# A new instruction order for an agent-attention and maxout-FFN kernel, with w_out loaded ahead of the second batch's keys

## The chip, the cores and the metric

The kernel runs on one core of one Trainium2 chip. The metric is the device time of one execution in microseconds (us), and less is better. Each time is a median over several executions on the chip.

The core has five engines, each with its own instruction stream that runs in order: TensorE (PE, matmuls; its weight loads are listed as PEld), VectorE (DVE), ScalarE (ACT), GpSimd (POOL) and SyncE (SP). SP computes nothing here: it issues all large DMA transfers, and its order is the order in which they enter the queue.

## What is computed

Two layers follow each other. Agent attention: 4 batches of 12,544 tokens with 128 channels; 49 agents per batch first gather from keys and values, then the queries read from the agents. After that comes a feed-forward layer whose hidden units are the maximum of three products.

```python
def sm(a, b):
    s = scale * (a @ b.transpose(0, 2, 1))
    s = s - s.max(-1, keepdims=True)
    e = np.exp(s)
    return e / (e.sum(-1, keepdims=True) + 1e-09)
a2k = sm(agents, k)
agent_v = a2k @ v
q2a = sm(q, agents)
x = (q2a @ agent_v).reshape(B * S, D)
...
h = np.maximum(np.maximum(x @ w1, x @ w2), x @ w3)
return (h @ w_out).astype(np.float32)
```

w1, w2 and w3 are 128 x 768, w_out is 768 x 128. Inputs and output are float32; the kernel multiplies in bfloat16.

## The kernel before

**Algebra.** The queries' side never forms x. For each batch the kernel multiplies the 49 agent values by w3 - w1 and w2 - w1 and by w1 times w_out once (the tile G), and each query tile's 49 exponentials then go straight to the hidden units. The maximum of three becomes a linear part and two ReLU-like steps.

**Steps.** The function `graph` names every step. Its names are used below, with a batch b and a chunk g for keys and values (12 chunks in batch 0, 11 in each later one), or a query tile s (49 tiles of 1,024 queries, so-called superblocks) and a sixth f of the hidden units.

- SP: `kl`, `vl` load a chunk of keys or values; `ql.s` a tile of queries; `lw..` half of a weight; `lwo` w_out; `st.s` stores a result tile; `kt` (batches 1 to 3) and `qd.s` transpose cast keys or queries by DMA.
- POOL: `kc`, `vc`, `qc` cast what was loaded to bfloat16 (L335, L517), `cwo` casts w_out (L405), `ea` sums exponentials (L474).
- PE: `ks` key scores (L359), `kv` exponentials times values (L376), `qt.s` transposes queries where DMA does not (L523), `sc.s` query scores (L533), `su` their sums (L545), `u.s.f` and `v.s.f` the two products for a sixth of the hidden units (both L558, two matmuls each, on half of the array's rows at a time), `li` the linear part (L582), `p.s.o.f` the output product (L592, four matmuls each), `pl` w1 times w_out (L417).
- ACT: `kx` and `ex` exponentials (L365, L539), `a.s.f` the first ReLU (L571, and L565 for f = 4), `x.s.4` (L568).
- DVE: `x.s.f` the maximum (L574), `ov` scales by the reciprocal sums and fills a result tile (L599), `qe` evacuates transposed queries (L527), `nr` normalises a batch's agent values (L428 for batch 0).

On PE the steps are of three kinds, set by the `mode` in `graph`: `u` and `v` use half of the rows (49 agents in each half), `sc` and the products for G half of the columns, all others the full array.

**Stages.** Batch 0's keys and values come first; its G is ready at some 41 us. From then on the superblocks 0 to 48 follow each other, overlapped, and the key and value chunks of batches 1 to 3 ride on the superblocks ahead of their own (batch 1 on superblocks 1 to 11, batch 2 on 12 to 22, batch 3 on 24 to 34).

**What sets the order.** Nothing is scheduled when the kernel is built: a string, `ORDER`, lists all 2,889 steps, and the function `run` issues them one after the other, each on its engine. A word is a step and, behind the slash, the buffers that its new tiles take; a step waits, beside its inputs, for the last reader of what its buffer held. The number of buffers is fixed:

```python
SLOTS = {"UV": 3, "OM": 2, "LD": 13, "QB": 3, "KB": 3, "VB": 4, "KT": 3, "QT": 3, "EQ": 4, "EK": 4, "AS": 3,
         "R": 13, "RC": 4, "OS": 9, "G": 4, "VA": 2, "EA": 2, "ES": 2, "KR": 2}
```

LD holds loaded chunks, tiles and weights; KB, VB and QB their casts; KT and QT what was transposed; EK and EQ exponentials; UV and OM are in PSUM, the matmuls' output; R holds hidden units, OS result tiles.

```python
for name in order:
    o = plan.ops[plan.index[name]]
    for t in o["new"]:
        self.new(plan.tiles[t], t)
    o["fn"]()
```

Of the kernel before, what the change touches and what calls it, by code (L numbers as in the profile page):

```python
# [25 lines left out]
TURNED = (*range(13, 36, 2), 26, 32, *range(36, 49))  # L26
# [89 lines left out]
def graph(plan, em):  # L116
# [93 lines left out]
    for s in range(NQ):  # L210
# [433 lines left out]
kl0.5/0 prep kl0.0/1 kl0.9/2 kl0.1/3 kl0.6/4 vl0.0/5 vl0.11/6 ql.0/7 kl0.2/8 kl0.10/9 kl0.7/10 kc0.1/0 vl0.5/11 kc0.9/1 kt0.1/0  # L644
lw3a/12 kc0.5/2 vl0.7/3 kc0.0/0 kt0.5/1 kl0.4/2 ke0.5/0 kc0.6/2 vl0.9/0 ke0.1/1 ks0.5/1 qc.0/0 kt0.0/2 kx0.5/0 kl0.8/1 vc0.0/0
kl0.11/4 qt.0/0 ke0.0/0 ks0.1/1 qe.0/0 ks0.0/2 kc0.7/0 kl0.3/7 kx0.1/1 kt0.6/0 vc0.5/1 vl0.6/5 sc.0/0 ke0.6/0 kc0.2/2 vl0.8/10
kt0.7/1 ex.0/0 kt0.2/0 ke0.7/1 vc0.7/2 vl0.10/11 ks0.7/1 kx0.0/2 kc0.4/2 vl0.2/8 kx0.7/3 kt0.9/2 wm.0/1 wm.1/1 vc0.11/3 kc0.10/0
ke0.9/1 vl0.4/3 vd0.11 ks0.9/2 ke0.2/2 to0.0/0 to0.7 kv0.0 vl0.3/9 kc0.8/1 kt0.10/0 to0.5 vc0.9/0 ks0.2/1 ke0.10/1 vl0.1/6 kv0.5
kt0.4/0 kc0.11/0 kx0.9/0 kv0.7 ke0.4/2 kx0.2/2 lw1a/2 kc0.3/2 to0.2 ks0.6/0 ks0.4/1 kx0.6/3 kt0.3/2 lw2a/4 vc0.6/2 kt0.8/0 to0.6
ke0.8/2 kv0.6 lw1b vc0.8/1 ke0.3/0 ks0.8/0 to0.9 lw3b kv0.9 vc0.10/2 kt0.11/2 to0.1 kx0.8/0 ke0.11/2 to0.8 vd0.10 kv0.8 lw2b  # L650
# [4 lines left out]
ex.1/1 x.0.5/1 kc1.2/1 qt.2/1 x.0.4/2 vl1.0/9 u.0.0/0 ql.3/8 qe.2/0 v.0.3/1 a.0.0/2 vl1.1/10 u.1.5/2 x.0.3/3 sc.2/1 gl/0 a.1.5/0  # L655
v.0.0/0 kc1.1/2 x.0.0/4 u.0.2/1 gvl v.1.5/2 a.0.2/1 li.0.0/0 kt1.1/2 p.0.0.3 x.1.5/5 p.0.0.1 ex.2/2 u.1.3/0 v.0.2/1 a.1.3/2
p.0.0.5 kt1.2/0 x.0.2/6 ks1.0/1 p.0.0.0 u.1.2/2 kx1.0/1 v.1.3/0 vc1.0/0 a.1.2/0 kl1.3/5 p.0.0.4 x.1.3/7 u.2.5/1 vl1.2/3 p.0.0.2
a.2.5/1 su.1 kl1.4/11 kv1.0 qc.3/0 u.1.1/2 ov.0.0/0 ql.5/9 v.1.2/0 a.1.1/2 vl1.4/2 u.1.4/1 re.1/1 va1.0/0 x.1.2/8 li.0.1/0 qt.3/1
kl1.8/8 vc1.1/0 a.1.4 p.0.1.4 u.1.0/2 qe.3/0 v.1.1/0 qc.4/0 a.1.0/0 v.1.4 x.1.1/2 p.0.1.1 vl1.3/4 p.0.1.5 p.0.1.3 x.1.4/0 p.0.1.2
p.0.1.0 u.2.3/0 ov.0.1 u.2.4/2 a.2.3/2 v.1.0/1 ks1.1/1 x.1.0/4 li.1.0/0 p.1.0.2 a.2.4 su.2 p.1.0.3 p.1.0.5 re.2/0 v.2.5/0 kx1.1/0  # L660
u.2.1/1 v.2.4 x.2.5/6 a.2.1/0 p.1.0.4 kv1.1 p.1.0.1 p.1.0.0 x.2.4/3 va1.1 v.2.1/0 ov.1.0/1 v.2.3/1 vc1.2/0 sc.3/1 x.2.3/1 u.2.2/2
ex.3/0 li.1.1/0 p.1.1.4 kc1.3/1 a.2.2/1 p.1.1.2 x.2.1/0 ks1.2/1 p.1.1.0 v.2.2/1 kx1.2/3 kc1.4/2 u.2.0/2 kt1.3/0 p.1.1.5 x.2.2/4
a.2.0/2 kv1.2 su.3 p.1.1.1 p.1.1.3 kl1.5/11 u.3.5/0 re.3/2 va1.2 v.2.0/1 ov.1.1 vl1.5/5 a.3.5/1 u.3.1/2 li.2.0/1 ql.6/3 x.2.0/7
p.2.0.3 p.2.0.4 kl1.6/6 a.3.1/0 qt.4/0 ql.7/10 u.3.4/0 qe.4/0 kt1.4/2 u.3.3/1 a.3.4 v.3.5/2 p.2.0.5 x.3.5/2 p.2.0.2 p.2.0.0
a.3.3/2 vc1.3/0 p.2.0.1 kl2.1/12 sc.4/0 ov.2.0/2 v.3.4 ex.4/1 v.3.3/2 ea1.0/0 v.3.1/1 x.3.4/5 x.3.3/8 li.2.1/1 vl2.0/7 p.2.1.5
ks1.3/0 su.4 p.2.1.4 kx1.3/1 x.3.1/6 u.3.2/0 u.4.5/2 a.3.2/2 kv1.3 p.2.1.3 kc1.5/1 p.2.1.0 va1.3 re.4/1 v.3.2/1 a.4.5/0 u.3.0/0
# [197 lines left out]
```

## Time and profile before

| | us |
|---|---|
| three runs | 447.28, 449.17, 452.19 |
| median | 449.17 |
| the profiled execution | 448.96 |
| its span, first to last instruction | 447.1 |

The page of the profile gives busy times by engine, 40 slices of the span, DMA queues and the costliest groups of instructions. The timeline gives stretches of instructions merged by group: start, duration, engine, line, operation, output and inputs, shapes, count, and in brackets the idle time of the engine before it with what ended it. "issue" is idle time for which the profile shows no wait. PE's matmuls overlap, and their ends are modelled, so that a group's pace is read from start to start. KB are 1,024 bytes.

From records of the waits, the engines' longest in total:

```
engine line waited for: us in total, times, longest us
POOL QB L517 <- DMA LD<-in_q_dram: 50.3, 8, 11.9
POOL KB L335 <- DMA LD<-in_k_dram: 42.8, 13, 8.4
PEld L592 <- issue: 41.1, 149, 0.6
POOL QB L517 <- DMA QT<-QB: 35.6, 8, 10.1
```

### The profile page before, as it was taken

To read this page: it belongs to the slowest core of one execution; us is meant where nothing else is said; L and a number is where in the kernel's file an instruction comes from. 1 tells how busy PE (TensorE), PEld (TensorE's weight loads), DVE (VectorE), ACT (ScalarE), POOL (GpSimd) and SP (SyncE) were. 2 spreads that over 40 slices of the span, in tenths; PEclk is the share of its full clock that TensorE was granted. 3 is DMA by queue.
4 is the path that set the end of the run, shared out by engine and by line. 5 is a ranking of instruction groups with operands and counts; after the bars stand their busy time and mean duration, and the time that the engine had idled before them with its cause. 6 is when DMAs were issued, how large, how long until landed. Compare 5 with 4: busy or idle time off the path is not lost.

```text
span 447.1 us, 12853 instructions
## 1 busy us (share of the span) xinstructions
PE 421.8 (94%) x5260; PEld 270.8 (61%) x5260; DVE 392.1 (88%) x496; ACT 393.6 (88%) x461; POOL 169.5 (38%) x176
## 2 busy tenths in 40 slices
PE   0787899999999999999899999999999999999996
PEld 0554466666666666666566666666665555655675
DVE  1345799999999999999899999998999999999996
ACT  1469799999999999999889999999999999999983
POOL 1641645555694222824871324527601201000000
PEclk9989699999999999999999999999999999999999
DMA  8999999999999999999999999999699464450405
GB/s 312 410 408 387 346 372 281 298 405 308 327 291 307 352 285 285 345 310 225 321 354 253 313 302 345 303 221 353 189 300 282 103 189 122 90 195 22 164 37 202
DMA packets 97045, 121.98 MB, mean 273 GB/s; under 512 B 70423, under 2 KB 73179, under 8 KB 96987
## 3 DMA queue, kind: packets, MB, share of 16 engines
q1 hardware_dynamic: 96784, 121.07, 90.4%
q8 instruction: 41, 0.67, 0.6%
q14 instruction: 17, 0.14, 0.1%
q10 hardware_dynamic: 203, 0.10, 0.1%
HBM read 78.74 MB, written 25.69 MB: 234 GB/s over the span
## 4 chain that ended last, share of the span: by engine, by line
PE 83%; DMA 8%; DVE 3%; issue 2%; POOL 2%; ACT 1%; SPq 1%; DVEq 0%; POOLq 0%
PE UV L558 35%; PE OM L592 31%; PE OM L582 6%; DMA LD<-in_v_dram 4%; PE OM L533 3%; DVE R L574 2%; PE OM L523 2%; DMA LD<-in_k_dram 2%; PE OM L376 2%; PE OM L359 2%; DMA LD<-in_q_dram 1%; PE OM L545 1%; SPq L325 1%; DVE OS L599 1%; POOL QB L517 1%
## 5 line engine op out<-in xcount | busy, mean ns | idle before, releaser
L574 DVE TENSOR_TENSOR R<-UV,AS 128x1024 bf16<-128x1024 f32 x245 | 293.4, 1219 | 17.8 <-PE UV L558 12.9
L571 ACT ACTIVATE AS<-UV 128x1024 bf16<-128x1024 f32 x245 | 246.3, 1024 | 17.8 <-PE UV L558 13.5
L558 PE MATMUL UV<-EQ,G 49*128 49x512 bf16 (+1 forms) x1248 | 181.7, 371 | 0.9
L592 PE MATMUL OM<-wo_bf,R 128*128 128x128 bf16 x2352 | 180.4, 220 | 0.0
L592 PEld LDWEIGHTS <-R 128*128 128x128 bf16 x2352 | 139.8, 98 | 43.4 <-issue 41.1
L558 PEld LDWEIGHTS <-G 49*128 49x128 bf16 x1248 | 61.5, 94 | 61.8 <-issue 21.7
L517 POOL CAST QB<-LD 128x1024 bf16<-128x1024 f32 x49 | 51.1, 1048 | 98.4 <-DMA LD<-in_q_dram 50.3
L335 POOL CAST KB<-LD 128x1152 bf16<-128x1152 f32 (+2 forms) x45 | 49.7, 1116 | 60.4 <-DMA LD<-in_k_dram 42.8
L599 DVE TENSOR_TENSOR OS<-OM,RC 128x512 f32<-128x512 f32 x98 | 67.1, 684 | 3.6 <-PE OM L592 2.5
L335 POOL CAST VB<-LD 128x1152 bf16<-128x1152 f32 (+1 forms) x33 | 37.3, 1137 | 47.7 <-DMA LD<-in_v_dram 14.7
L565 ACT ACTIVATE UV<-UV 128x1024 f32<-128x1024 f32 x49 | 49.8, 1017 | 2.5 <-PE UV L558 1.2
L568 ACT ACTIVATE R<-UV 128x1024 bf16<-128x1024 f32 x49 | 50.1, 1023 | 1.7 <-PE UV L558 1.2
L582 PE MATMUL OM<-G,EQ 128*128 128x256 bf16 x196 | 37.9, 276 | 0.0
L539 ACT ACTIVATE EQ<-OM 128x512 bf16<-128x512 f32 x49 | 29.5, 602 | 0.9 <-PE OM L533 0.6
L474 POOL TENSOR_TENSOR EA<-EA,EK 128x441 f32<-128x441 f32 x27 | 27.6, 1023 | 4.8 <-ACT EK L365 4.1
L347 DVE COPY KT<-UV 128x1152 bf16<-128x1152 bf16 (+1 forms) x12 | 8.2, 700 | 17.3 <-PE UV L342 17.3
L582 PEld LDWEIGHTS <-EQ 128*128 128x128 bf16 x196 | 12.6, 97 | 15.6 <-issue 14.2
L533 PE MATMUL OM<-QT,agT 128*64 128x512 bf16 (+1 forms) x104 | 20.4, 398 | 0.2 <-DMA QT<-QB 0.2
L365 ACT ACTIVATE EK<-OM 128x441 bf16<-128x441 f32 (+1 forms) x33 | 17.8, 540 | 2.9 <-POOL EA L474 1.6
L376 PE MATMUL OM<-EK,VB 128*128 128x49 bf16 x392 | 17.3, 186 | 2.7 <-ACT VB L333 1.4
L359 PEld LDWEIGHTS <-KT 128*128 128x128 bf16 x392 | 14.6, 98 | 7.5 <-issue 4.5
L376 PEld LDWEIGHTS <-VB 128*128 128x128 bf16 x392 | 14.3, 97 | 7.9 <-issue 5.0
(67 smaller groups left out, 186.1 us busy)
## 6 DMA issues: line engine op xcount, KB each, us to landing
LD<-in_q_dram SPq DMA_DIRECT2D x48, 512.0 KB, 6.4
out_dram<-OS SPq DMA_DIRECT2D x48, 512.0 KB, 5.6
LD<-in_k_dram SPq DMA_DIRECT2D x40, 576.0 KB, 7.3
LD<-in_v_dram SPq DMA_DIRECT2D x40, 576.0 KB, 8.7
LD<-in_k_dram SPq DMA_DIRECT2D x3, 512.0 KB, 9.0
LD<-in_v_dram SPq DMA_DIRECT2D x3, 512.0 KB, 8.1
LD<-in_moe_w_dram SPq DMA_DIRECT2D x6, 192.0 KB, 8.4
KT<-KB SPq DMA_TRANSPOSE x33, 7.0
```

What stands on the lines that cost most here:

```text
L335: (self.nc.gpsimd if eng == POOL else self.nc.vector).tensor_copy(out=out, in_=src)
L376: self.nc.tensor.matmul(out, vb[:, j, :], e[:, j * A:(j + 1) * A], start=False, stop=True, skip_group_check=True)
L517: return lambda: self.nc.gpsimd.tensor_copy(out=self.t[f"qb.{s}"], in_=self.t[f"q.{s}"][:, :GT, :])
L533: self.nc.tensor.matmul(self.t[f"qs.{s}"][h * H:(h + 1) * H, jj * P:(jj + pairs) * P], self.agT[:, b, :], self.t[f"qT.{s}"][:, 2 * jj + h: ...
L558: self.nc.tensor.matmul(t[:, h, jj * P:(jj + pairs) * P], self.t[f"G{b}"][h * H:h * H + A, c + f * P:c + (f + 1) * P], self.t[f"e.{s}"][h ...
L565: return lambda: self.nc.scalar.activation(self.t[f"u.{s}.{f}"], self.t[f"u.{s}.{f}"], AF.Relu)
L568: return lambda: self.nc.scalar.activation(self.t[f"r.{s}.{f}"], self.t[f"u.{s}.{f}"], AF.Relu)
L571: return lambda: self.nc.scalar.activation(self.t[f"a.{s}.{f}"], self.t[f"u.{s}.{f}"], AF.Relu)
L574: return lambda: self.nc.vector.tensor_tensor(out=self.t[f"r.{s}.{f}"], in0=self.t[f"v.{s}.{f}"], in1=self.t[f"a.{s}.{f}"], op=ALU.max)
L582: self.nc.tensor.matmul(self.t[f"o.{s}.{o}"][:, i * 2 * C:(i + 1) * 2 * C], self.t[f"e.{s}"][:, jj * P:(jj + 1) * P], self.t[f"G{of[jj]}"] ...
L592: self.nc.tensor.matmul(self.t[f"o.{s}.{o}"][:, c:c + C], self.t[f"r.{s}.{f}"][:, h, jj * P:(jj + 1) * P], self.wo_bf[:, f, :], start=Fals ...
L599: self.nc.vector.tensor_tensor(out=self.t[f"os.{s}"][:, j:j + 4, :], in0=self.t[f"o.{s}.{o}"].rearrange("p (j c) -> p j c", c=C), in1=self ...
```

## The change

The operations, their engines and sizes and the number of buffers stay as they are; so does which query tiles are transposed by DMA (`TURNED` is only written with other spaces). The string `ORDER` is replaced: the steps stand in another order, and many take other buffers. The last 271 words are the same. The part around the end of batch 0 and the start of the superblocks, before and after:

```diff
@@ -641,195 +641,196 @@
 ORDER = """
-kl0.5/0 prep kl0.0/1 kl0.9/2 kl0.1/3 kl0.6/4 vl0.0/5 vl0.11/6 ql.0/7 kl0.2/8 kl0.10/9 kl0.7/10 kc0.1/0 vl0.5/11 kc0.9/1 kt0.1/0
-lw3a/12 kc0.5/2 vl0.7/3 kc0.0/0 kt0.5/1 kl0.4/2 ke0.5/0 kc0.6/2 vl0.9/0 ke0.1/1 ks0.5/1 qc.0/0 kt0.0/2 kx0.5/0 kl0.8/1 vc0.0/0
...
-vc0.2/0 su.0/1 ks0.3/2 ks0.11/0 kx0.4/0 kv0.2 ql.1/11 vc0.4/1 to0.4 ks0.10/1 kx0.3/2 kv0.4 kl1.0/8 kx0.11/3 to0.3 kx0.10/0 vc0.3/1
-to0.10 to0.11 wm.2/2 wm.3/0 wm.4/1 rc0/0 lwo/3 vc0.1/0 kv0.3 kv0.11 ql.2/9 d31a kv0.10 d21a kl1.2/10 kv0.1 wm.5/2 wm.6/0 cw1
-ql.4/6 nr0/0 d31b kl1.1/5 gpa/1 gpc/0 wm.7/2 gva d32 gpb/2 gvc u.0.1/1 gvb tw1/0 a.0.1/0 d21b qc.1/0 u.0.3/2 ew1 gpd/0 a.0.3/1
-u.0.5/1 gvd cwo qt.1/0 re.0/0 a.0.5/2 v.0.1/0 kc1.0/0 qe.1/0 u.0.4/2 pl/1 x.0.1/0 a.0.4 v.0.5/1 qc.2/0 kt1.0/1 sc.1/0 el v.0.4
...
+kx0.10/1 ke0.4/1 ks0.4/1 vc0.6/0 to0.10 ks0.2/0 kv0.6 kx0.2/0 ex.0/0 to0.2 kv0.2 kx0.8/2 kt0.3/0 vl0.1/4 lw3a/0 lw1a/3 lw1b
+lw2a/11 lw3b lw2b ql.1/6 qc.1/0 lwo/12 cwo ql.2/5 qc.2/1 vc0.8/2 to0.8 wm.0/2 wm.1/2 kv0.8 vc0.10/0 vd0.10 kx0.4/0 vc0.4/2 ke0.3/0
...
+to0.3 wm.3/1 wm.4/2 wm.5/0 rc0/0 d31a cw1 kv0.3 kv0.10 wm.6/1 wm.7/2 kv0.1 nr0/0 gpa/0 gva d21a gpc/1 gvc d31b u.0.1/0 a.0.1/0 d32
...
```

So SP's queue around w_out changes from `ql.1 kl1.0 lwo ql.2 kl1.2 ql.4 kl1.1 kt1.0 vl1.0` to `ql.1 lwo ql.2 vl1.0 kl1.1 kl1.0 kl1.2 vl1.2 ql.3 vl1.1 kt1.0`. Further on the two orders differ in which loads, stores and transposes SP issues first, for instance ahead of the last transpose of batch 2's keys (`kt2.10`): `kt2.9 qd.21 ql.24 st.14 vl3.5 st.13 kt2.10` before, `vl3.0 ql.23 vl3.2 st.4 ql.26 kt2.10` after; in where POOL's `ea` sums stand among the casts; and in how `u`, `v`, `p` and the small steps alternate on PE.

More of the change, by code (lines that the diff above doesn't have):

```diff
@@ L25 @@
 LATER = [KT] * 10 + [8]
-TURNED = (*range(13, 36, 2), 26, 32, *range(36, 49))
+TURNED = (*range(13,36,2),26,32,*range(36,49))
 PE, ACT, DVE, POOL, SP = range(5)
@@ L728 @@
-p.18.1.5 a.19.0/2 p.18.1.3 p.18.1.0 va2.8 u.20.3/2 ov.18.1 v.19.0/0 kl3.2/8 a.20.3/0 u.20.4/1 x.19.0/7 su.20 li.19.0/1 p.19.0.2
-kc3.0/1 st.9 p.19.0.3 a.20.4 p.19.0.1 re.20/2 u.20.1/2 v.20.5/0 vc3.1/0 a.20.1/2 v.20.4 x.20.5/4 p.19.0.5 kt3.0/2 p.19.0.4
-p.19.0.0 x.20.4/9 vc2.10/2 sc.21/0 ov.19.0/6 v.20.3/2 u.20.2/0 ex.21/0 v.20.1/1 ea2.6 x.20.3/8 ks2.9/1 a.20.2/1 li.19.1/0 p.19.1.4
-ea2.7 p.19.1.5 x.20.1/5 su.21 p.19.1.2 kx2.9/2 u.21.3/0 v.20.2/2 qc.23/2 a.21.3/0 kv2.9 x.20.2/1 u.20.0/1 p.19.1.3 vc3.2/1
@@ new lines @@
+kt2.5/0 re.14/0 va2.2 u.14.5/2 a.14.5/2 st.12 vl2.6/7 vc2.3/1 u.14.4/1 a.14.4 li.13.0/0 p.13.0.2 p.13.0.3 p.13.0.1 st.10 v.14.5/2
+x.14.5/9 u.14.1/0 a.14.1/0 sc.15/1 ex.15/1 ea2.0/0 vc2.4/2 ea2.1 ea2.2 p.13.0.4 p.13.0.5 p.13.0.0 ov.13.0/3 v.14.4 x.14.4/7
+v.14.3/2 x.14.3/6 v.14.1/0 x.14.1/0 ks2.3/1 su.15 kx2.3/0 li.13.1/0 p.13.1.0 p.13.1.3 vl2.7/6 kl2.9/3 kl2.6/12 vl2.5/0 vc2.5/0
+u.14.2/1 kc2.6/1 a.14.2/1 u.14.0/2 a.14.0/0 p.13.1.5 p.13.1.1 kv2.3 va2.3 re.15/2 v.14.2/0 x.14.2/2 u.15.5/1 a.15.5/2 p.13.1.4
@@ new lines @@
+p.14.1.5 ov.14.1 u.16.4/0 a.16.4 v.15.0/1 x.15.0/9 kt2.6/1 u.16.5/2 a.16.5/2 sc.17/1 ex.17/2 kt2.9/2 li.15.0/0 p.15.0.3 p.15.0.2
+p.15.0.1 v.16.5/1 ql.22/10 v.16.4 x.16.4/6 u.16.2/2 a.16.2/0 qc.19/2 qd.19/0 vl2.9/11 p.15.0.4 p.15.0.5 x.16.5/7 p.15.0.0
+ov.15.0/2 ks2.5/1 v.16.3/1 x.16.3/0 u.16.1/0 su.17 li.15.1/0 ea2.3 kc2.8/0 ea2.4 vc2.6/2 p.15.1.0 p.15.1.3 a.16.1/2 v.16.1/2
+x.16.1/5 u.16.0/1 u.17.5/0 p.15.1.4 p.15.1.2 kx2.5/2 kv2.5 re.17/0 va2.5 a.16.0/1 a.17.5/2 ea2.5 vc2.8/0 p.15.1.5 p.15.1.1 ov.15.1
@@ new lines @@
+u.17.4/1 v.16.2/2 x.16.2/4 li.16.0/1 p.16.0.5 p.16.0.1 v.16.0/0 x.16.0/8 a.17.4 v.17.4 x.17.4/1 u.17.3/2 a.17.3/0 kc2.7/2 vc2.7/1
+qt.18/0 qe.18/1 p.16.0.4 v.17.5/1 x.17.5/3 u.17.1/0 a.17.1/1 p.16.0.0 p.16.0.3 p.16.0.2 ov.16.0/0 sc.18/0 ex.18/1 v.17.3/2
+x.17.3/9 u.17.2/0 a.17.2/2 v.17.1/1 x.17.1/2 ks2.6/0 kx2.6/2 li.16.1/1 p.16.1.0 ea2.6 qc.20/2 p.16.1.1 qc.22/0 u.17.0/0 a.17.0/0
+v.17.2/2 x.17.2/5 kv2.6 p.16.1.5 vc2.9/2 kc2.10/1 su.18 va2.6 re.18/2 u.18.5/1 a.18.5/1 v.17.0/0 x.17.0/7 st.9 p.16.1.3 p.16.1.2
@@ new lines @@
+x.21.5/0 sc.22/1 ex.22/0 p.20.0.2 p.20.0.5 p.20.0.0 ov.20.0/4 u.21.1/1 a.21.1/2 v.21.3/2 x.21.3/8 u.21.2/0 a.21.2/1 li.20.1/1
+p.20.1.4 kt2.10/0 ks2.10/0 v.21.1/1 x.21.1/2 p.20.1.2 kx2.10/3 ql.24/2 vc2.10/0 ea2.7 u.22.5/2 a.22.5/0 v.21.2/0 x.21.2/5 p.20.1.0
+p.20.1.3 u.21.0/1 a.21.0/2 kv2.10 su.22 qc.23/1 vc3.1/2 ea2.8 ea2.9 fo2/0 to2 qd.23/0 kl3.0/0 ql.27/9 u.22.4/2 a.22.4 va2.10
+nr2/0,2 kc3.0/1 vc3.6/0 re.22/0 u.22.3/0 v.21.0/1 x.21.0/9 p.20.1.5 li.21.0/0 vl3.3/11 p.21.0.2 p.21.0.4 p.20.1.1 ov.20.1 a.22.3/1
@@ L833 @@
+p.48.1.0 ov.48.1 st.48
 """
```

349 lines of the change are left out of this document (170 added, 179 removed).

## The prediction

> **What bounds the kernel now.** I read the page's first lines, then the windows, then single stretches of the timeline.
>
> ```profile
> span 447.1 us, 12853 instructions
> ...
> PE 421.8 (94%) x5260; PEld 270.8 (61%) x5260; DVE 392.1 (88%) x496; ACT 393.6 (88%) x461; POOL 169.5 (38%) x176
> ...
> PEclk9989699999999999999999999999999999999999
> ```
>
> ```profile
> 20.00:40.00 20.00, 15.57 (x256) 10.78 (x254) 7.93 (x17) 15.29 (x23) 5.15 (x6) 0.91 1.03 403
> 41.00:58.00 17.00, 15.13 (x131) 7.31 (x130) 12.98 (x18) 13.51 (x18) 9.74 (x9) 0.80 1.09 341
> 60.00:100.00 40.00, 39.99 (x542) 26.96 (x541) 37.88 (x49) 37.87 (x46) 21.24 (x21) 1.00 1.05 339
> 180.00:220.00 40.00, 38.65 (x506) 25.45 (x507) 37.26 (x47) 37.35 (x45) 24.43 (x25) 1.00 1.10 297
> 260.00:300.00 40.00, 39.98 (x516) 25.88 (x513) 37.75 (x46) 38.07 (x46) 15.19 (x15) 1.00 1.10 300
> 320.00:340.00 20.00, 19.97 (x240) 12.41 (x238) 18.74 (x24) 17.86 (x23) 4.46 (x5) 1.00 0.96 281
> 340.00:400.00 60.00, 59.60 (x616) 33.99 (x615) 57.37 (x63) 57.25 (x64) 7.29 (x7) 1.00 0.55 145
> ```
>
> The columns of a window are its length, then busy time of PE, PEld, DVE, ACT and POOL, the granted clock, the DMA share and GB/s. Four stages stand there. Up to about 40 us the loads set the pace (DMA share 1.03 at 403 GB/s). From 41 to 58 nothing is full: ACT is idle 17.00 - 13.51 = 3.5 us, DVE 4.0 us, and the clock is 0.80. From 60 to 300 PE has hardly a gap and the DMA share in the rows shown lies between 1.05 and 1.10: two resources are full at once. After 340 the DMA share is 0.55, and PE alone is left. Whether a busy PE is really a full PE is seen in the timeline:
>
> ```profile
> 250.28 0.62 PE L592 MATMUL OM<-wo_bf,R 128*128 128x128 bf16 x8
> ...
> 250.83 0.39 PE L558 MATMUL UV<-EQ,G 49*128 49x512 bf16 x2
> 251.15 0.45 PEld L592 LDWEIGHTS <-R 128*128 128x128 bf16 x8 [0.23 <-issue]
> 251.15 0.62 PE L592 MATMUL OM<-wo_bf,R 128*128 128x128 bf16 x8
> ...
> 251.61 0.40 PE L376 MATMUL OM<-EK,VB 128*128 128x49 bf16 x9
> ...
> 251.93 0.83 PE L558 MATMUL UV<-EQ,G 49*128 49x512 bf16 x6
> ...
> 252.70 0.39 PE L582 MATMUL OM<-G,EQ 128*128 128x256 bf16 x2
> ```
>
> Read starts against starts. Eight L592 matmuls before another of the full-array kind (L376) take 251.61 - 251.15 = 0.46 us; before an L558, which uses half the rows, 250.83 - 250.28 = 0.55. One L558 pair before a full-array matmul takes 0.32; three pairs take 0.77, so that the two inner ones take (0.77 - 0.32) / 2 = 0.225. A **switch between kinds costs about 0.095 us** either way, and the rest goes from start to start with no room. PE is at its own pace here, and the count of switches is part of the time.
>
> At this point a rule stands against mine. The Trainium skill (Perfetto Trace Analysis, Identifying the Most-Contended Engine) says that matmul busy time misjudges TensorE and that weight-load busy time should be taken instead. By it PE, at 61%, would have room, ACT and DVE would be the contended engines, and the switches would cost nothing. The row with "0.23 <-issue" speaks against it here: the weight load's idle time sits inside the switch. I keep it as a rival.
>
> **The change, part by part.** *First keys and values.* Counted in the order of SP's instructions, 23 key and value loads, the first q tile and one half of w3 stand ahead of the last values; afterwards the same without w3.
>
> ```profile
> LD<-in_q_dram SPq DMA_DIRECT2D x48, 512.0 KB, 6.4
> out_dram<-OS SPq DMA_DIRECT2D x48, 512.0 KB, 5.6
> LD<-in_k_dram SPq DMA_DIRECT2D x40, 576.0 KB, 7.3
> ...
> LD<-in_moe_w_dram SPq DMA_DIRECT2D x6, 192.0 KB, 8.4
> ```
>
> At 403 GB/s a key or value load (576 KB, 0.590 MB) takes 1.46 us of the queue, a q or result tile 1.30, half a weight 0.49. The last values, their normalisation (39.64 below) and the first product over hidden units (41.15) come 0.5 us earlier: **-0.5**.
>
> *The passage into the steady state.*
>
> ```profile
> 39.64 0.21 DVE L428 TENSOR_TENSOR avT<-OM,KR 128x49 bf16<-128x49 f32 x1 [0.20 <-PE OM L376]
> ...
> 41.15 0.39 PE L558 MATMUL UV<-EQ,G 49*128 49x512 bf16 x2
> ...
> 44.56 0.83 POOL L405 CAST wo_bf<-LD 128x768 bf16<-128x768 f32 x1 [1.39 <-DMA LD<-in_moe_w_out_dram]
> 45.33 1.15 POOL L335 CAST KB<-LD 128x1152 bf16<-128x1152 f32 x1
> 45.44 0.49 PE L417 MATMUL OM<-wo_bf,w1T 128*128 128x128 bf16 x6 [1.05 <-POOL wo_bf L405]
> ...
> 46.42 1.04 POOL L517 CAST QB<-LD 128x1024 bf16<-128x1024 f32 x1
> ...
> 47.52 1.03 PE L523 MATMUL OM<-ident,QB 128*128 128x128 bf16 x8 [0.60 <-POOL QB L517]
> ...
> 49.13 1.94 ACT L571 ACTIVATE AS<-UV 128x1024 bf16<-128x1024 f32 x2 [0.99 <-PE UV L558]
> ```
>
> Now SP sends q tile 1, keys 1.0, w_out, q tile 2. Afterwards it sends q 1, w_out, q 2, then batch 1's values and keys: w_out and q 2 land one key load, 1.46 us, earlier, and the key cast at 45.33 no longer stands between the two casts on POOL that PE waits for. The three waits shown, 1.05 + 0.60 + 0.99 = 2.64 us, go; PE's wait for w_out was 1.05, less than the 1.46 gained, and next late there is DVE's evacuation of w1, ahead of which u.0.0 and v.0.5 now stand as cover. The bounds are nothing and the 3.5 us that ACT is idle, which hold the half clock's price too; I take **-2.6**, the named waits. What pays is batch 1's first transpose, which has three more key or value loads ahead of it (4.4 us). Its consumer ks1.0 stands behind 14 u, 13 v and 15 p steps instead of 8, 7 and 3: 12 pairs and 12 groups of four L592 at about 0.225 are 5.4 us of PE. That covers it; without the cover up to 4.4 us would show.
>
> *Kinds on PE.* From u.0.1 on I count 577 switches before and 597 after: 14 of the extra ones by the end of batch 2's part, 20 in all. The last 181 PE steps are the same in both. **+1.9**, of which 1.3 by 220 us.
>
> *The wait at 217.*
>
> ```profile
> 213.27 2.62 SPq L454 DMA_TRANSPOSE KT<-KB  x1
> ...
> 216.57 0.54 ACT L365 ACTIVATE EK<-OM 128x441 bf16<-128x441 f32 x1 [1.55 <-POOL EA L474]
> ...
> 217.16 0.39 PE L376 MATMUL OM<-EK,VB 128*128 128x49 bf16 x9 [1.14 <-ACT EK L365]
> ```
>
> ACT's exponentials for keys 2.9 waited for POOL, whose sum ea2.6 stood behind casts of keys and values. Afterwards ea2.6 stands about 6 us of PE steps, added up at the durations above, ahead of that use instead of 1.3, so this goes: **-1.5**. What is late next is ks2.10, the last keys of batch 2.
>
> ```profile
> 223.48 0.37 PE L359 MATMUL OM<-agT,KT 128*128 128x49 bf16 x8
> ```
>
> ```profile
> DMA to landing us min/median/max: 7.1/8.2/8.6
> ```
>
> That second row is of the KT transposes between 195 and 226 us. The one issued at 213.27 landed at about 213.27 + 8.2 = 221.5, 2.0 us before its use at 223.48. After the change PE would be there 0.5 + 2.6 + 1.5 - 1.3 = 3.3 us earlier, at 220.2. But SP has 75 key or value loads, 27 q loads and 13 stores ahead of this transpose, where it had 74, 25 and 14, with the same 26 transposes: one load of 1.46 and one tile of 1.30 more, 2.8 us. With the DMA share at 1.10 there is no idle time to put them into. So PE waits 221.5 - 220.2 = 1.3 us if the two transfers overlap the turn, and 4.1 if they delay it in full. I take the middle, **+2.7**.
>
> The sum: -0.5 - 2.6 + 1.9 - 1.5 + 2.7 = 0.0, between -1.4 and +1.4 by the last term alone. The profiled execution took 448.96 us, 1.9 above its span and 0.2 below the median of the three runs, 449.17. So the forecast is **449.0**: what the start gains, the switches and the full DMA queue give back.
>
> **The rivals.** *The lead is kept.* The transposes come in time for the earlier PE, and the gain passes 220 us without a wait: 0.0 - 2.7 = -2.7 in all, **446.3**; with the whole 3.5 us of ACT's idle time won, 445.4. For it: each transpose could be issued sooner, since SP's order around it is new. Against it: the share of 1.10.
>
> *PE has room.* By the page named above, the 1.9 us of switches are not paid: **447.1**.
>
> *The fetches.* The change weighs four places of the instruction fetches.
>
> ```profile
> q8 instruction: 41, 0.67, 0.6%
> ```
>
> These are 41 packets of 16 KB. In this profile PE's named waits after 44 us are 1.05, 0.60 and 1.14, and each has another cause, so no fetch shows. The three runs differ by 4.9 us; if that is the fetches, an order that rides them out falls to the lowest run's 447.28: **447.3**. The Trainium skill (Runtime: NRT & Kernel Launch, Instruction fetch mechanics) says that crossing a 16 KB block is mostly hidden. By that, this part of the change does nothing, which is the case in which it does not do what it says.
>
> *Slower: the result tiles.*
>
> ```profile
> DVE OS L599 <- DMA out_dram<-OS: 0.3, 1, 0.3
> ```
>
> There are nine result tiles, and SP stores them late to leave the queue to loads. Now DVE waited for a store once, 0.3 us. When PE reaches ks2.3, 13 tiles are done in both orders; SP has 6 stores ahead of the transpose for it before, 4 afterwards, so up to nine tiles are held, all there are, less those that SP stores in between. A store takes 5.6 us to land; where it is issued less than that ahead, DVE's scaling waits, then the two OM tiles, then PE. It decides from the point where SP runs one transfer (1.30 us) later than now while nine are held. From superblock 12 to 32, if one in four pays 1.3 us, 5 x 1.3 = 6.5: **455.5**.
>
> **How the numbers follow.** Forecast 0.54; lead kept 0.20; PE has room 0.06; fetches 0.06; result tiles 0.14. About 1% (4.5 us) is what a measurement here tells from no change. Below 444.7 lies only the end of the lead-kept case with an earlier, warmer passage: 0.11. Above 453.7 lies most of the result-tile case: 0.13. Within, 0.76. The range reaches through the lead-kept case, with another 1.4 us (the spread of the last term) off its 445.4, to 444.0, and on the other side to three waits of 1.3 us for a store beyond the forecast's own upper end, 448.96 + 1.4 + 3.9 = 454.3.
>
> **What would show it.** Right: the first L558 near 40.7; ACT's idle time in 41 to 58 below 1.5 us; no wait of PE for the w_out cast; PE's wait for a transpose of K near 220 us and no wait of ACT for EA there; steps from start to start as quoted. Wrong: ACT still idle 3 us in the passage, with the clock again at half (PEclk has a 6 in that slice now); or L599 waiting for stores between 150 and 320; or PE waiting for K or q transposes at many places, which would mean that the queue's order costs more than the two transfers counted.

## The result, and the profile after

| | before | after |
|---|---|---|
| median of 14 runs each, us | 449.17 | 446.06 |
| range, us | 446.49 to 452.19 | 445.03 to 447.75 |
| profiled execution, us | 448.96 | 445.74 |
| its span, us | 447.1 | 443.6 |

The ratio is 0.9935, 95% interval 0.9915 to 0.9954: the new order is 2.9 us faster by the ratio, 3.1 by the medians. That lies in the range, and where I had put the likeliest case (449.0) it is the rival "the lead is kept" (446.3) that came true. The page of after begins:

```profile
span 443.6 us, 12856 instructions
...
PE 420.9 (95%) x5260; PEld 269.4 (61%) x5260; DVE 393.4 (89%) x496; ACT 393.6 (89%) x461; POOL 169.4 (38%) x176
...
PEclk9999999999999999999999999999999999999999
```

The same work in a shorter span, and the 6 in the clock row is gone. The windows of after, with the columns as in the prediction:

```profile
41.00:58.00 17.00, 16.41 (x160) 8.63 (x159) 15.79 (x19) 16.67 (x22) 8.31 (x8) 1.00 1.08 336
60.00:100.00 40.00, 39.91 (x537) 25.76 (x535) 38.01 (x53) 37.91 (x46) 23.45 (x23) 1.00 1.13 351
...
340.00:400.00 60.00, 59.63 (x618) 34.34 (x615) 57.39 (x64) 57.34 (x65) 7.28 (x7) 1.00 0.53 140
```

In the passage ACT is idle for 17.00 - 16.67 = 0.3 us where it was 3.5, DVE for 1.2 where it was 4.0, and the clock is 1.00 where it was 0.80. From 60 us on the rows look as before. PE's timeline in the passage:

```profile
40.69 0.39 PE L558 MATMUL UV<-EQ,G 49*128 49x512 bf16 x2
...
44.48 0.51 PE L417 MATMUL OM<-wo_bf,w1T 128*128 128x128 bf16 x6
...
47.02 0.62 PE L523 MATMUL OM<-ident,QB 128*128 128x128 bf16 x8
...
47.89 0.39 PE L582 MATMUL OM<-G,EQ 128*128 128x256 bf16 x2
```

None of these rows has a bracket: the waits of 1.05 and 0.60 us for w_out and for q tile 2 are gone, and the first output step (L582) starts 4.2 us earlier than in before's timeline:

```profile
52.05 0.61 PE L582 MATMUL OM<-G,EQ 128*128 128x256 bf16 x2
```

Now the place where I had expected the gain to be given back, after's timeline around ks2.10:

```profile
205.57 7.14 SPq L454 DMA_TRANSPOSE KT<-KB  x1
...
219.28 0.37 PE L359 MATMUL OM<-agT,KT 128*128 128x49 bf16 x8
...
224.27 0.39 PE L582 MATMUL OM<-G,EQ 128*128 128x256 bf16 x2 [0.57 <-DVE RC L550]
```

ks2.10 runs at 219.28 without a bracket, 4.2 us earlier than in before (223.48). SP began its transpose at 205.57 instead of 213.27, but was on it for 7.14 us instead of 2.62, so that the issue ended at 212.71 instead of 215.89. When SP began, six transfers ahead of it were still out, in before three. It landed at 219.24, in before at 221.39. That is 2.15 us earlier; the rest of PE's 4.2 us of lead comes out of the 2.09 us of slack that this transpose had in before. Now the slack is gone: 0.04 us lie between landing and use, as in the cases below where PE did wait for a transpose, and the step began 0.05 us later behind its predecessor than this pair of steps usually takes. So the lead passes here with nothing to spare. A new wait of 0.57 us, for a reciprocal from DVE, stands behind it.

To see where the difference lies I took from before's trace the lower quartile of the distances from start to start, for each kind of PE step and of its successor, and added these up along either order; what a trace takes beyond that is PE's lost time. It is a reading of one execution each, and how finely the steps are sorted moves an entry by up to some 1.4 us and a difference by some 0.5.

| part | before | after | difference |
|---|---|---|---|
| first hidden product starts, us | 41.15 | 40.69 | -0.5 |
| PE's steps at their own pace, us | 382.1 | 384.1 | +2.0 |
| lost between 40 and 60 us | 5.3 | 1.3 | -4.0 |
| lost everywhere else | 14.0 | 12.9 | -1.1 |

The sum, -3.6, is the difference of the spans, -3.5, up to rounding. So the gain is made before 60 us (what is won elsewhere, 1.1 us, doesn't pay the 2.0 of the switches), and the question is why it is still there at the end.

### The profile page after: what moved, and what is told of

Its sections match the earlier page's. It is cut to its first block, busy times and chain, and to the rows that moved or that the text cites. A ratio compares the mean times of both kernels' runs of the same rounds, so it can differ in the third digit from the quotient of the medians.

```text
span 443.6 us, 12856 instructions
## 1 busy us (share of the span) xinstructions
PE 420.9 (95%) x5260; PEld 269.4 (61%) x5260; DVE 393.4 (89%) x496; ACT 393.6 (89%) x461; POOL 169.4 (38%) x176
## 4 chain that ended last, share of the span: by engine, by line
PE 87%; ACT 4%; DVE 3%; DMA 2%; issue 2%; SPq 0%; POOL 0%; ACTq 0%; DVEq 0%; POOLq 0%
PE UV L558 35%; PE OM L592 32%; PE OM L582 6%; PE OM L533 4%; PE OM L376 2%; DMA LD<-in_k_dram 2%; ACT AS L571 2%; PE OM L359 2%; PE OM L523 2%; PE UV L342 2%; DVE R L574 1%; PE OM L545 1%; ACT VB L333 1%; PE UV L439 1%; DVE KT L347 1%
## 5 line engine op out<-in xcount | busy, mean ns | idle before, releaser
L558 PE MATMUL UV<-EQ,G 49*128 49x512 bf16 (+1 forms) x1248 | 181.6, 368 | 1.8 <-DVE R L574 0.3
L558 PEld LDWEIGHTS <-G 49*128 49x128 bf16 x1248 | 59.9, 93 | 60.7 <-issue 20.2
L517 POOL CAST QB<-LD 128x1024 bf16<-128x1024 f32 x49 | 50.8, 1040 | 118.3 <-DMA LD<-in_q_dram 47.1
L599 DVE TENSOR_TENSOR OS<-OM,RC 128x512 f32<-128x512 f32 x98 | 66.9, 683 | 2.8 <-PE OM L592 1.9
L582 PE MATMUL OM<-G,EQ 128*128 128x256 bf16 x196 | 37.8, 275 | 0.6 <-DVE RC L550 0.6
L582 PEld LDWEIGHTS <-EQ 128*128 128x128 bf16 x196 | 12.4, 97 | 17.9 <-issue 16.8
L333 ACT ACTIVATE VB<-LD 128x1152 bf16<-128x1152 f32 (+1 forms) x12 | 12.1, 1042 | 9.0 <-DMA LD<-in_v_dram 9.0
L359 PEld LDWEIGHTS <-KT 128*128 128x128 bf16 x392 | 14.6, 98 | 6.7 <-issue 4.3
```

The source lines that it names most:

```text
L517: return lambda: self.nc.gpsimd.tensor_copy(out=self.t[f"qb.{s}"], in_=self.t[f"q.{s}"][:, :GT, :])
L558: self.nc.tensor.matmul(t[:, h, jj * P:(jj + pairs) * P], self.t[f"G{b}"][h * H:h * H + A, c + f * P:c + (f + 1) * P], self.t[f"e.{s}"][h ...
L582: self.nc.tensor.matmul(self.t[f"o.{s}.{o}"][:, i * 2 * C:(i + 1) * 2 * C], self.t[f"e.{s}"][:, jj * P:(jj + 1) * P], self.t[f"G{of[jj]}"] ...
L599: self.nc.vector.tensor_tensor(out=self.t[f"os.{s}"][:, j:j + 4, :], in0=self.t[f"o.{s}.{o}"].rearrange("p (j c) -> p j c", c=C), in1=self ...
```

## The experiments

Each set of runs shares its runs of before on the same chip; ratios are to those, with 95% intervals. The 14 runs of after were made beside other runs of before than those of the experiments, whose medians lie between 447.99 and 448.76; so a difference of medians to after is less sure than one of ratios, and where the two differ both are given. Where an order is put together from two, the buffers behind the seam are chosen anew: of the free ones, the one freed earliest. "Feed" means the instructions of SP and POOL: loads, stores, transposes, casts and sums of exponentials.

**1. The start of after with the rest of before, and the reverse.**

```diff
 x_start: words 1 to 344 of after (up to li.2.0)
-         the other words in after's order
+         the other words in before's order
 x_rest:  words 1 to 340 of before (up to li.2.0)
-         the other words in before's order
+         the other words in after's order
```

> The order of after up to the first output tile of superblock 2 (about 53 us), then the remaining steps in the order of before. Theory 'start' (the whole gain is made before 60 us and is kept by any order behind it): 587 switches instead of 597 save 0.95 us, the wait of before at 217 us may come back with 1.1, so about 446 us (444.5 without that wait), and PE reaches the last keys of batch 2 (ks2.10) some 4.5 us before the 223.5 us of before without waiting for their transpose. Theory 'queue' (the step of my prediction: the DMA queue has no idle time, so that transpose cannot land earlier than its 221.4 us): PE waits about 2.4 us at ks2.10, and the time is 448 or more. Theory 'rest' (the new order of the steady part brings the gain): 449, no better than before.

> The order of before up to the first output tile of superblock 2 (about 57 us), then the remaining steps in the order of after. Theory 'start': the passage keeps its waits and its half clock, 589 switches cost 1.1 us more than in before, the wait at 217 (1.1) may go, so 449 to 450 us, with ACT idle some 3.5 us in 41 to 58 us. Theory 'rest': 446.

x_start took 448.89 us, ratio 1.0004 (0.9978 to 1.0031): as slow as before, although its start is after's. PE's timeline of x_start shows where the lead went:

```profile
72.08 0.40 PE L359 MATMUL OM<-agT,KT 128*128 128x49 bf16 x9 [0.71 <-DMA KT<-KB]
...
81.43 0.40 PE L359 MATMUL OM<-agT,KT 128*128 128x49 bf16 x9 [0.39 <-DMA KT<-KB]
...
189.67 0.40 PE L359 MATMUL OM<-agT,KT 128*128 128x49 bf16 x9 [0.50 <-DMA KT<-KB]
...
225.09 0.42 PE L491 MATMUL OM<-ES,ones 128*128 128x49 f32 x2 [0.97 <-POOL ES L485]
```

The same two steps in before, without waits:

```profile
74.11 0.39 PE L359 MATMUL OM<-agT,KT 128*128 128x49 bf16 x9
...
82.90 0.39 PE L359 MATMUL OM<-agT,KT 128*128 128x49 bf16 x9
```

The transpose for the second (kt1.4) landed at 80.86 us in before and at 81.39 in x_start. SP's timeline of x_start has it as

```profile
70.37 5.86 SPq L454 DMA_TRANSPOSE KT<-KB  x1
```

SP began it 1.9 us earlier than in before (72.29) and was done with it at 76.23 instead of 75.96. The earlier PE doesn't bring it forward. In all five traces with before's feed (before, x_start and, below, after_feed_b, b_wout and b_warm) it landed between 80.55 and 81.39; with after's feed (after, x_start_feed, a_nowout) between 73.28 and 75.32. In before it had 2.0 us of slack, so no more than that can be won there. Theory "start" falls; "queue" holds, at other transposes than the one that I had named.

x_rest took 453.47, ratio 1.0119 (1.0086 to 1.0152), more than either theory gave. It meets new waits at its own seam, as PE's timeline shows:

```profile
70.81 0.39 PE L558 MATMUL UV<-EQ,G 49*128 49x512 bf16 x2 [0.52 <-DVE R L574]
...
72.31 0.39 PE L558 MATMUL UV<-EQ,G 49*128 49x512 bf16 x2 [1.11 <-ACT AS L571]
...
74.09 0.49 PE L558 MATMUL UV<-EQ,G 49*128 49x512 bf16 x2 [1.38 <-DVE R L574]
```

Besides, the clock is at half for 6.8 us from 46.9 and for 3.4 us from 74.2 in its trace. That makes it no clean test of the rest of after, and what after's feed is worth behind the start of before was not measured otherwise; by the table above it could win no more than 1.1 us there. The run shows one thing: 7.95 us behind after at superblock 4, it is 7.8 behind at superblock 44. PE makes up nothing.

**2. Two parts of the passage alone, in before.**

```diff
 b_wout, SP's order and POOL's order:
-ql.1 kl1.0 lwo ql.2 kl1.2          qc.1 cwo kc1.0 qc.2
+ql.1 lwo ql.2 kl1.0 kl1.2          qc.1 cwo qc.2 kc1.0
 b_warm, ahead of L417 (n = 4) and of q tile 2's transposes (n = 2):
+        for _ in range(n):
+            self.nc.tensor.matmul(self.t[name], self.ident, self.ident.unsqueeze(1).to_broadcast([P, 4, P]), start=True, stop=True, ...)
```

> Before with one edit: the load of the first keys of batch 1 (kl1.0) behind those of w_out and q tile 2, and its cast behind theirs on POOL. Theory 'w_out alone' (the passage is slow because w_out and q tile 2 land 1.46 us too late): PE's waits of 1.05 and 0.60 us fall below 0.3 in all, the clock no longer falls to half, and the time is 445.5 to 447. Theory 'the whole start' (the waits move to the next late piece, w1's evacuation on DVE and the steps on ACT in before's order): the waits go but ACT stays idle over 2.5 us in 41 to 58 us, time 448 to 449.

> Before with six extra matmuls of 128x512 on constants, whose output is overwritten: four ahead of the product of w1 and w_out (L417), two ahead of the transposes of q tile 2 (L523), where PE waits 1.05 and 0.60 us. Theory 'clock' (the half clock from 47.1 to 54.0 us comes of PE's idle time between 44.4 and 47.5, and costs ACT's idle time of 48 to 54 us, 2.1 us by the windows): the granted clock stays 1.00 in 41 to 58, the first output steps come 1.5 to 2.5 us earlier though both waits stay, time 447. Theory 'waits' (the late w_out and q tile set the pace, the clock costs nothing): clock 1.00, time 449.

b_wout: 447.72 us, ratio 1.0000 (0.9980 to 1.0021). b_warm: 448.95, ratio 1.0016 (0.9992 to 1.0039). The windows of 41 to 58 us, b_wout first:

```profile
41.00:58.00 17.00, 15.54 (x161) 8.31 (x161) 15.04 (x21) 15.72 (x22) 10.57 (x10) 1.00 1.08 329
```

```profile
41.00:58.00 17.00, 16.07 (x159) 8.56 (x157) 15.11 (x21) 15.46 (x21) 9.84 (x10) 1.00 1.11 321
```

In both profiles the clock is 1.00 here. For b_warm, whose order is before's, the price of the half clock can be read: from the first hidden product to ks1.0, in b_warm (L566 there is L558) and then in before, where the product starts at 41.15:

```profile
42.05 0.39 PE L566 MATMUL UV<-EQ,G 49*128 49x512 bf16 x2
...
53.03 0.39 PE L359 MATMUL OM<-agT,KT 128*128 128x49 bf16 x9
```

```profile
54.45 0.39 PE L359 MATMUL OM<-agT,KT 128*128 128x49 bf16 x9
```

10.98 us against 13.30: the half clock cost 2.3 in this execution. It is not the rule. 6.8 us at half clock make the mean granted clock 0.992 or less, which 15 of the 98 runs of before made beside the experiments have (median 450.30 us; the other 83: 448.09), and none of after's 14. So a profile of b_wout or b_warm without the half clock doesn't show that the edit kept it away, and b_warm's median could gain by the clock in few runs only. For the profiled executions, theory "clock" is right about the passage, b_wout's lead shows that w_out is right too (they are largely the same loss), and neither lead lasts to the end. The lead over before's trace, at the second output tile of superblock 0 and at the first of superblock 44 (starts of L582), shows it for all these kernels, in us. The first of the two steps doesn't stand at the same place in the two starts, so the work of PE between them differs too; it is counted at PE's own pace, as above, with its extra switches:

| kernel | feed behind the start | lead at 0 | lead at 44 | of the loss, more work between | lost otherwise |
|---|---|---|---|---|---|
| b_wout | before | 2.4 | 0.3 | 0 | 2.1 |
| b_warm | before | 1.4 | -0.4 | 0 | 1.8 |
| x_start | before | 5.1 | 0.9 | 1.8 | 2.4 |
| after_feed_b (next) | before | 4.3 | 0.5 | 2.6 | 1.2 |
| x_start_feed (next) | after | 2.7 | 1.2 | 1.8 | -0.3 |
| a_nowout (below) | after | 3.3 | 1.8 | 2.6 | -1.1 |
| after | after | 5.1 | 3.5 | 2.6 | -0.9 |

**3. The feed alone.** SP's and POOL's instructions behind the start change places between the two orders; PE, ACT and DVE stay. In x_start_feed they come in after's order, in after_feed_b in before's. A piece of SP's order:

```diff
 x_start_feed (after_feed_b is the reverse, on after):
-kt1.3 kl1.5 vl1.5 ql.6 kl1.6 ql.7 kt1.4 kl2.1 vl2.0 kt1.5
+kt1.3 kl1.6 kt1.4 vl1.4 kl1.5 kl1.8 kt1.6 vl1.5 ql.7 kt1.5
...
```

> The kernel x_start (start of after, then before's order) with the instructions of SP and POOL behind the start in after's order: PE, ACT and DVE run before's order, loads, stores, casts and transposes come in after's. Theory 'order of the feed' (the DMA queue moves the same bytes by the same times in all these kernels, and a lead is kept where the transposes stand ahead of the loads that PE does not need yet): PE's waits for transposes of K at 72, 81, 107, 190 and 225 us go, the lead of some 4 us at 50 us is still above 3 at 300 us, time 445 to 446. Theory 'PE order' (after's PE order needs the transposes later, its feed order is not better): the waits stay or turn up at other transposes, 448 to 450.

> The reverse: after, with the instructions of SP and POOL behind the start in the order of before (as they stand in x_start). Theory 'order of the feed': the lead is given back at K transposes, PE waits 2 us or more for them between 70 and 110, time 449 or more. Theory 'PE order': the lead is kept, 446.

x_start_feed: 446.56 us, ratio 0.9963 (0.9938 to 0.9988). after_feed_b: 449.50, ratio 1.0032 (1.0011 to 1.0053). With after's feed the start's lead is kept under before's PE order, and with before's feed it is lost under after's. The second half is clear by the ratios (after: 0.9915 to 0.9954). In the first the interval overlaps a little with x_start's, and the lead was not "above 3 at 300 us" as expected: this execution began late, had only 2.7 us at superblock 0, and lost nothing of it beyond its extra work. In x_start_feed the rows of x_start with "DMA KT<-KB" stand without a bracket; in after_feed_b's timeline one such wait takes most of what is lost:

```profile
81.02 0.40 PE L359 MATMUL OM<-agT,KT 128*128 128x49 bf16 x9 [1.94 <-DMA KT<-KB]
```

It is the transpose kt1.4 again. SP's own timeline, before and then after, shows why (start, time on SP, operation):

```profile
67.08 1.30 SPq L454 DMA_TRANSPOSE KT<-KB  x1
68.50 1.61 SPq L325 DMA_DIRECT2D LD<-in_k_dram  x1
70.15 0.43 SPq L325 DMA_DIRECT2D LD<-in_v_dram  x1
70.62 0.43 SPq L513 DMA_DIRECT2D LD<-in_q_dram  x1
71.10 0.67 SPq L325 DMA_DIRECT2D LD<-in_k_dram  x1
71.81 0.44 SPq L513 DMA_DIRECT2D LD<-in_q_dram  x1
72.29 3.67 SPq L454 DMA_TRANSPOSE KT<-KB  x1
```

```profile
65.64 1.36 SPq L454 DMA_TRANSPOSE KT<-KB  x1
67.71 0.34 SPq L325 DMA_DIRECT2D LD<-in_k_dram  x1
68.09 1.85 SPq L454 DMA_TRANSPOSE KT<-KB  x1
```

Before sends five loads between two transposes that PE needs 9 us apart, after sends one. Nothing had been moved faster by then: by 140 us 55 chunks of keys and values, some 18 q tiles and 4 result tiles had landed in before, after, x_start and b_wout alike. From 60 to 300 us a transfer is always out in these traces. So up to there it is the order, not the amount moved, that decides whether the next thing that PE needs is in front. Later the queue of after does move more, at the same DMA share (the last two figures are the share and GB/s; before, then after):

```profile
140.00:212.00 72.00, 71.86 (x929) 46.43 (x926) 68.34 (x86) 69.34 (x83) 29.04 (x28) 1.00 1.08 300
```

```profile
140.00:212.00 72.00, 71.67 (x920) 46.06 (x919) 68.18 (x84) 68.42 (x80) 36.10 (x35) 1.00 1.07 318
```

That is 1.3 MB more, over two loads of keys. So a share above 1 didn't mean that nothing more could be moved; which part of the order earns this was not tested.

**4. Some transposes by hand.**

```diff
 x_min, SP's order in x_start:
-vl1.4 kl1.8 vl1.3 kt1.3 kl1.5 vl1.5 ql.6 kl1.6 ql.7 kt1.4
+vl1.3 kt1.3 kt1.4 vl1.4 kl1.8 kl1.5 vl1.5 ql.6 kl1.6 ql.7
```

> x_start with three instructions of SP moved: the transpose of keys 1.4 directly behind that of keys 1.3 (ahead of five loads), and two loads (values 1.4, keys 1.8) behind both. Theory 'these transposes are the loss': the waits of 0.88 and 0.55 us at keys 1.3 and 1.4 go and stay gone, 447. Theory 'the whole feed paces': both go, but the transpose of keys 1.7, bound by a late load and cast, still lands near 107 us, and PE waits 1 to 2 us there; time 448 to 449.

451.48 us, ratio 1.0060 (1.0031 to 1.0089): slower than either theory. Both waits went, and PE's timeline has a larger one instead:

```profile
79.06 0.99 PE L523 MATMUL OM<-ident,QB 128*128 128x128 bf16 x8 [2.03 <-POOL QB L517]
```

SP stood in front of kt1.3 until its cast was done at 65.9 us, with the loads now behind it, so that what POOL casts ahead of q tile 5 came late. This profile also has the clock at half for 3.4 us from 41.6, ahead of the edit, and for 3.4 us from 79.1, at the end of the wait of 2.03; five of its twelve runs have a mean clock of 0.992 or less, so the 451 is not all the doing of the transposes. Three moves don't make after's feed.

**5. The switches.**

```diff
 PE's order, superblocks 35 to 47, one of 20 places of a_more, then two of the moves of a_less:
-p.36.0.4 p.36.0.5 u.37.1 v.37.5
+p.36.0.4 u.37.1 p.36.0.5 v.37.5
...
-p.35.0.3 u.35.0 v.35.2 p.35.0.4 p.35.0.5 u.36.5 p.34.1.0 p.34.1.2 u.36.3
+p.35.0.3 p.35.0.4 p.35.0.5 p.34.1.0 p.34.1.2 u.35.0 v.35.2 u.36.5 u.36.3
```

a_few has 26 moves of a_less's kind over superblocks 1 to 47.

> After with 20 steps of L592 between superblocks 35 and 47 moved behind the next hidden step, so that PE changes between full and half rows 40 times more often (637 switches instead of 597), at a place where the DMA queue is half empty. Theory 'PE is full' (0.095 us a switch): PE's steps from the move on end 3.7 us later, 449.8. Theory 'PE has room' (weight loads 61% busy): 446, no change.

> After with L592 steps between superblocks 35 and 47 moved ahead of the hidden steps in front of them where their input has long been there: 44 switches fewer (553). Theory 'PE is full and alone': 4.1 us earlier, 442.0. Theory 'ACT and DVE at 95% of the stretch are next': most of it is lost in waits of PE for the buffers that they free, 444 to 446. Theory 'PE has room': 446.

> After with L592 steps moved ahead of hidden steps in front of them at 26 places from superblock 1 to 47, only where no run of hidden steps gets longer than three, which is the count of UV buffers (in a_less, runs of four to six each cost PE 0.85 to 1.3 us behind them, runs of up to three hardly anything): 545 switches instead of 597. Theory 'switches cost as long as the UV buffers last': 4.9 us less PE time, of which up to 2 come back as waits, 441 to 443. Theory 'after is at the pace of ACT and DVE': 446, or more.

| kernel | switches | us | ratio | against after, medians | against after, ratios |
|---|---|---|---|---|---|
| a_more | 637 | 449.71 | 1.0039 (1.0019 to 1.0060) | +3.7 | +4.7 |
| a_less | 553 | 454.39 | 1.0135 (1.0108 to 1.0162) | +8.3 | +9.0 |
| a_few | 545 | 451.87 | 1.0092 (1.0072 to 1.0113) | +5.8 | +7.1 |

a_more is 3.65 us for 40 switches by the medians and 3.9 along its trace from superblock 30 to the end, 0.09 to 0.10 each, as read from the starts. The Trainium skill (Perfetto Trace Analysis, Identifying the Most-Contended Engine) would judge TensorE's room by its weight loads, 61% busy here, and by the share of peak arithmetic, which I did not work out; by the weight loads alone a_more would have stayed at 446, and the run speaks against that for this kernel. But the price works one way only. In the other direction the row of the hidden products, in the groups of 300 to 440 us, tells what happened, in after and then in a_less (the last figure but the releasers is the idle time ahead of them):

```profile
L558 PE MATMUL UV<-EQ,G 49*128 49x512 bf16 (+1 forms) x492 | 66.8, 349 | 0.8 <-DVE R L574 0.3
```

```profile
L558 PE MATMUL UV<-EQ,G 49*128 49x512 bf16 (+1 forms) x428 | 64.2, 368 | 10.9 <-ACT AS L571 5.4 <-DVE R L574 2.9 <-ACT R L568 0.7
```

Hidden products next to each other wait for ACT and DVE to free their three UV buffers. In a_less each run of four or more was followed by 0.85 to 1.3 us of lost time, and I took "not over three" for the rule; that it would come out slower than after stood in none of its theories. a_few kept to the rule and lost all the same: 24.4 us beyond PE's own pace instead of 14.2, where its steps alone were 4.9 us shorter. Theory "switches cost as long as the UV buffers last" falls. ACT and DVE are busy for 57.3 and 57.4 of the 60 us in after's row of 340 to 400, so they have little room for products that come sooner. That PE's changes of kind space the hidden products at the pace that ACT and DVE can take is my reading of these rows; no run tests it by itself.

**6. The named part of the change undone alone.**

```diff
 a_nowout, SP's order and POOL's order in after:
-ql.1 lwo ql.2 vl1.0 kl1.1 kl1.0          qc.1 cwo qc.2 kc1.0
+ql.1 kl1.0 lwo ql.2 vl1.0 kl1.1          qc.1 cwo kc1.0 qc.2
```

> After with its named part undone alone: the load of batch 1's first keys (kl1.0) ahead of w_out and q tile 2 again, and its cast on POOL between theirs. Theory 'w_out carries the passage': w_out and q tile 2 land 1.46 us later, PE waits about 1.1 us for the w_out cast and again for the q tile, ACT's idle time in 41 to 58 us grows from 0.3 to 2 or more, and since after's order keeps what it has, the time is 448 to 449. Theory 'the rest of the start covers it' (u.0.0 and v.0.5 stand as cover ahead): below 0.5 us of ACT's idle time more, 446 to 447.

447.49 us, ratio 1.0005 (0.9978 to 1.0031): no faster than the runs of before beside it. That is 3.1 us above after by the ratios, 1.4 by the medians; at the end of its trace it is 1.7 behind, 0.45 of which is a later first product. The waits came back, in PE's timeline:

```profile
46.03 0.49 PE L417 MATMUL OM<-wo_bf,w1T 128*128 128x128 bf16 x6 [1.11 <-POOL wo_bf L405]
...
48.88 0.62 PE L523 MATMUL OM<-ident,QB 128*128 128x128 bf16 x8 [0.26 <-POOL QB L517]
```

ACT's idle time in 41 to 58 us rose to 1.6, not 2, and the clock stayed at 1.00 in this execution. By the traces w_out ahead of the keys is a third of the gain at the start, 1.25 us of 4.0; the rest is the new order around it, which has more PE work in hand while it waits. By the ratios it is the whole gain, give or take 1.5 us. One reason may be the clock: four of the twelve runs have a mean clock of 0.992 or less and take 449.27 to 451.75 us, the others at most 447.55, and no run of after has such a clock. What the part is worth stays open between these values.

**7. The places of the fetches.**

```diff
 a_shift, in k_turn:
+            if g == 6:
+                for _ in range(56):
+                    self.nc.tensor.matmul(self.flat("kT_ps0.6")[:, :2], self.ident, self.ident[:, :2], start=True, stop=True, ...)
```

> After with 56 extra matmuls of two columns ahead of the transposes of keys 0.6, where PE waits 3.1 us for a cast at 10.7 to 13.8 us; their output is overwritten. Every later PE instruction stands 112 places (a matmul and its weight load each) further on in the code, so PE's fetches come at other points of the work, with the order unchanged. Theory 'fetches' (their places are worth the spread of a few us): after 60 us PE has gaps that after has not, or loses those that it has, and the time moves by more than 1.5 us from 446.06. Theory 'fetches are hidden': from the first hidden product on PE's steps keep their distances within 0.5 us in all, time 445.5 to 446.6.

448.27 us, ratio 0.9989 (0.9961 to 1.0017), which doesn't overlap after's 0.9915 to 0.9954. PE's waits between 60 and 110 us, of which after has none there:

```profile
PE OM L527 <- POOL QB L521: 1.3, 1, 1.3
PE OM L363 <- DMA KT<-KB: 0.4, 1, 0.4
```

(L527 and L363 are L523 and L359.) No PE wait has a fetch for its end, and still the time rose by 2.2 us; "hidden" misses the time, "fetches" gives the size, and there are gaps as it named them, but behind both stands a transfer that came late. The first wait goes back to a load of keys (kl1.6) that landed at 74.99 us instead of 72.35, with the cast of q tile 5 behind its cast on POOL. It was late before it was issued. SP's timeline of a_shift, to be read against that of after under 3 (65.64 and 67.71; L458 is L454):

```profile
68.07 1.36 SPq L458 DMA_TRANSPOSE KT<-KB  x1
69.55 0.50 SPq L325 DMA_DIRECT2D LD<-in_k_dram  x1
```

The delay had grown along the queue: 0.7 us at the last load of batch 0 (38.18 against 37.49), 1.8 at q tile 4, 2.4 at the keys 1.3, whose cast SP needs for this transpose. Whether that is chance, as the starts of equal orders scatter by as much (last section), or has to do with the fetches, is not shown. The Trainium skill (Runtime: NRT & Kernel Launch, Instruction fetch mechanics) calls the crossing of a block mostly hidden; PE's rows agree, and why the time rose stays open.

## Why the prediction was right, and where it was wrong

**The step that failed** is the last term, "+2.7" at ks2.10: "With the DMA share at 1.10 there is no idle time to put them into. So PE waits". The queue was never empty, as assumed. But I added the two extra transfers to the landing time of before's trace, 221.5, as if SP reached this transpose at the old time and the queue could not have moved more by then. SP began it 7.7 us earlier and was done with it 3.2 us earlier, the queue had moved 1.3 MB more from 140 to 212 us, and it landed at 219.24, just in time for PE at 219.28. In the words of the rival: "each transpose could be issued sooner, since SP's order around it is new." The mechanism that I feared is real, in the feed of before: x_start, b_wout, b_warm and after_feed_b gave back 1.2 to 2.4 us of lead beyond their extra work. I had looked at one transpose of after's feed; after's trace shows that the feed as a whole lets the 4.2 us pass, at this transpose with no slack left, and x_start_feed that it does so for a smaller lead under the other PE order.

**The term that was mis-sized** is the passage, "-2.6", measured -4.0 in the two profiles. I added up three named waits, of which the third, 0.99, is ACT's behind PE's two and no further time of PE, and left the half clock, 2.3 us by b_warm, to the bound of -3.5, although the row with 0.80 was in front of me. The parts overlap, so the bound by ACT's idle time was the better value: it fell by 3.2. But the half clock is in few of before's executions, so that in most of them the passage has less to win.

**Right:** "+1.9" for the switches (2.0 along the two orders, and a_more's 0.09 to 0.10 each). "-1.5" for the wait at 217: the time lost between 200 and 220 us fell by 1.3; what came late next was 0.57 us for a reciprocal at 224, which I had not foreseen. The transposes of batch 1's keys, 4.4 us later in the queue, were covered as worked out: ks1.0 waited for nothing. "-0.5" for the first keys fits this pair of traces, but executions of one order scatter more than that (below), so it is not shown.

**The rivals.** The lead was kept: 446.3 against 446.06. That the figure fits so closely is partly luck: the passage won 1.4 us more than its sum has. And the 1% that I took for what can be told from no change was too much: the interval reaches 0.2% to either side. "PE has room" is refuted by a_more, although a_less and a_few show that PE is not alone at the limit. The result tiles cost nothing; the only row of L599 in after's list of waits is for PE, not for a store:

```profile
DVE OS L599 <- PE OM L592: 1.9, 6, 0.6
```

The fetches are left as above.

No version tried beats after: x_start_feed, with ten switches fewer, is at 446.56.

## What to carry to other kernels

A lead won at the start is kept only if the feed lets it through: where the DMA queue is full, look for each transfer's slack to its use, because an earlier engine can gain no more than the smallest slack and what the landing itself moves forward; the remedy here was the order in the queue. When you cost a transfer in a new order, work out anew when it is issued; don't add to its old landing time. And the price of a thing read in one direction (0.09 to 0.10 us for a switch more) need not be the gain of removing it, when the engines beside it are at 95%.

## What was not expected of the hardware

- **The same start, 3 us apart.** In the profiles of a_more and x_start_feed the same instructions up to 50 us put the first hidden product at 40.08 and 43.16 us; the last key or value chunk had landed at 37.05 and 38.90. With a full queue in front of everything, this scatter alone moves single runs by as much as the whole change.
- **A half clock for 6.8 us** (47.1 to 54.0 us in before) behind PE's waits of 1.05 and 0.60, in 15 of 98 runs of before at most. For 3.4 us it came at the end of a wait of 2.03 us in x_min (79.1 us) and behind waits of 1.11 and 1.38 in x_rest (74.2 us). In the profiles of b_warm, with six filler matmuls, and of a_nowout, with waits of 1.11 and 0.26, it did not come.
- **112 PE instructions more at an idle place** went with 2.2 us, though no PE wait is for its code.
